# A fused recurrence and expert kernel: the first 768 tokens by plain products, weight sums moved to the second block, first loads from three queues

## Chip, cores, metric

The kernel runs on one core of a Trainium2 chip. The metric is the device time of one execution in microseconds (us), lower is better. Runs are grouped into rounds in which a kernel and the kernel before run on the same chip.

## The reference, cut to what matters

```
sig = 1 / (1 + exp(-f_logit))                 # batch 4, sequence 6080, width 256
f = lower_bound + (1 - lower_bound) * sig
h[t] = f[t] * h[t-1] + (1 - f[t]) * x[t]      # the recurrence; its output y has 24320 rows
hid = y @ w_in                                # 256 -> 2048, w_in arrives in 64-bit floats
g = hid - tanh(hid)
out = g @ w_out                               # 2048 -> 256, w_out in 64-bit floats
```

## The kernel before

Tokens are handled in blocks: one of 256 and 47 of 512. A block has four units u (a quarter of the hidden width each). Both matrix products use a scheme of seven half-size products in place of eight (Winograd's form of Strassen's), which needs four sums of each weight and of the activations. VectorE (DVE) makes these sums, does the recurrence, and takes part in converting the weights from 64-bit patterns to fp32. TensorE (PE) multiplies, ScalarE (ACT) squares and copies, and SP issues the transfers.

Some words for what follows. A mix is one of the sums of activations that the scheme needs. A bank is a piece of PSUM, the memory that PE writes its products to. For g, ScalarE squares a product and forms a quadratic of the square, VectorE makes a factor of it and multiplies the product by that factor (the shrink). This polynomial serves for small values only, so a flag records whether a square was over 0.03, and a general version of the kernel then runs.

```python
def round_weight(n):                 # conversion, then the four sums of the scheme
    ...
    to_float32(dsts, raw[:], temps)  # 5 passes of 1024 columns on DVE, 2 on ScalarE
    A21 = S3                         # the slot of A21 is overwritten by S3
    for o, a, b, op in (
        (S1, A21, A22, ALU.add), (S2, S1, A11, ALU.subtract),
        (S4, A12, S2, ALU.subtract), (S3, A11, A21, ALU.subtract),
    ):
        nc.vector.tensor_tensor(out=w[:, o, :], in0=w[:, a, :], in1=w[:, b, :], op=op)
...
fetch_weight(order[0])               # all on nc.sync: w_in 0,
fetch(0)                             # f_logit and x of the first block (256 tokens),
... lower_bound ...
fetch_weight(order[1])               # w_in 1
...
def need(n):                         # convert and sum when the first product needs it
    while ready <= order.index(n):
        round_weight(order[ready])
        ...
for cycle in range(-1, NBLK + 3):    # one fixed interleaving of all steps of a block
    for name, u, at in turns:
        ...
        if name[0] in "PQ":
            need((int(name[0] == "Q"), u))
        steps[name](j * NU + u)
```

Of the kernel before, what the change touches and what calls it, by code (L numbers as in the profile page):

```python
# [8 lines left out]
FP32 = mybir.dt.float32  # L9
ALU = mybir.AluOpType  # L10
AF = mybir.ActivationFunctionType
# [3 lines left out]
BF16 = mybir.dt.bfloat16  # L15
PSUM = bass.MemoryType.PSUM
P = 128
# [3 lines left out]
TINY = 0.03  # L21
RA, RB, RC = 0.2302117198239662, -0.2895648714772302, 0.24948550042070589
# [8 lines left out]
def kernel(  # L31
# [25 lines left out]
    nc = tc.nc  # L57

    B, S, D = x.shape
    DFF = moe_w_in.shape[1]  # L60
    N = B * S
    KC = D // P
    TB = 512
    HB = TB // 2
    NQ = TB // P
    NU = DFF // TB
    H = 32
    G = P // H
    assert D == 2 * P and DFF == 4 * TB and N % HB == 0

    sizes = [HB] * (N % TB // HB) + [TB] * (N // TB)
    starts = [sum(sizes[:j]) for j in range(len(sizes))]
    NBLK = len(starts)
    srcs = [a.rearrange("b s d -> (b s) d") for a in (f_logit, x)]
# [2 lines left out]
    lb = const.tile([P, KC], FP32, name="lb")  # L77
    om = const.tile([P, KC], FP32, name="om")
    nom = const.tile([P, KC], FP32, name="nom")
    flags = const.tile([P, NBLK * NU * 2], FP32, name="flags")  # L80
# [4 lines left out]



    def fetch_w_in(u, raw):

        src = moe_w_in.rearrange(  # L90
            "(i k a) (s u f) -> i k u a s f", i=G, k=KC, a=H, s=2, u=NU
        )
        dst = raw.rearrange("p (k s f) -> p k s f", k=KC, s=2)
        for i in range(G):
            for k in range(KC):
                nc.sync.dma_start(out=dst[i * H : (i + 1) * H, k], in_=src[i, k, u])  # L96

    def fetch_w_out(u, raw):

        src = moe_w_out.rearrange("(s u c m) d -> u s m c d", s=2, u=NU, c=2, m=P)  # L100
        dst = raw.rearrange("p (s c d) -> p s c d", s=2, c=2)
        for s in range(2):
            nc.sync.dma_start(out=dst[:, s], in_=src[u, s])

    def to_float32(dsts, raw, temps):

# [117 lines left out]
    def fast(ctx):  # L224
# [8 lines left out]
        fetch, steps, ys = recurrence(ctx)  # L233
# [16 lines left out]
        A11, S3, A12, A22, S1, S2, S4 = range(7)  # L250
        raws = {}

        def fetch_weight(n):
            kind, u = n
            raw = rawpool.tile([P, KC * TB], INT64, name="raw")
            (fetch_w_in, fetch_w_out)[kind](u, raw[:])
            raws[n] = raw

        def round_weight(n):
            kind, u = n  # L260
            raw = raws.pop(n)
            temps = [
                rawpool.tile([P, 2, 2, HB], FP32, name=s, tag=s, bufs=1)[:] for s in "emr"
            ]
            w = (w_in, w_out)[kind][u]
            if kind == 0:
                dsts = [(w[:, 0:4, :].rearrange("p n f -> p (n f)"), lambda a: a)]
            else:
                dsts = [
                    (  # L270
                        w[:, 2 * s + k, :].rearrange("p (n a) -> p n a", a=H),
                        lambda t, s=s, k=k: t[:, s * TB : (s + 1) * TB].rearrange(
                            "p (n k a) -> p n k a", k=2, a=H
                        )[:, :, k],
                    )
                    for s in range(2)
                    for k in range(2)
                ]
            to_float32(dsts, raw[:], temps)
            A21 = S3  # L280
            for o, a, b, op in (
                (S1, A21, A22, ALU.add),
                (S2, S1, A11, ALU.subtract),
                (S4, A12, S2, ALU.subtract),
                (S3, A11, A21, ALU.subtract),
            ):
                nc.vector.tensor_tensor(  # L287
                    out=w[:, o, :], in0=w[:, a, :], in1=w[:, b, :], op=op
                )
# [27 lines left out]
        st = {}  # L317
# [98 lines left out]
        acc = {}  # L416
# [117 lines left out]
        for word in around.split():  # L534
            name, u, at = re.fullmatch(r"([a-zA-Z0-9]+)(?:\.(\d))?([+-]\d)?", word).groups()
            turns.append((name, u and int(u), int(at or 0)))


        order = [(0, u) for u in range(NU)] + [(1, u) for u in range(NU)]

        with tc.manual_schedule():
            nc.vector.memset(ones[:], 1.0)
            nc.vector.memset(zeros[:], 0.0)


            bank = ps_b.tile([P, 2, HB], FP32, name="B", tag="B")
            nc.tensor.matmul(
                bank[:], lhsT=zeros[:, 0:P], rhs=zeros[:], start=True, stop=True,
                skip_group_check=True,
            )  # L550
            fetch_weight(order[0])
            fetch(0)
            for i in range(G):
                nc.sync.dma_start(
                    out=lb[i * H : (i + 1) * H, :],
                    in_=lower_bound.rearrange("(i k a) -> i a k", i=G, a=H)[i],
                )
            fetch_weight(order[1])
            nc.vector.tensor_scalar(
                out=om[:], in0=lb[:], scalar1=-1.0, scalar2=1.0,  # L560
                op0=ALU.mult, op1=ALU.add,
            )
            nc.vector.tensor_scalar_add(out=nom[:], in0=lb[:], scalar1=-1.0)
            ready = 0

            def need(n):
                nonlocal ready
                while ready <= order.index(n):
                    round_weight(order[ready])
                    ready += 1  # L570
                    if ready + 1 < len(order):
                        fetch_weight(order[ready + 1])

            for cycle in range(-1, NBLK + 3):
                for name, u, at in turns:
                    j = cycle + at
                    if not 0 <= j < NBLK:
                        continue
                    if u is None:
                        steps[name](j)  # L580
                        if name == "tx" and j + 1 < NBLK:
                            fetch(j + 1)
                        continue
                    if name[0] in "PQ":
                        need((int(name[0] == "Q"), u))
                    steps[name](j * NU + u)
            nc.vector.reduce_max(out=worst[:], in_=flags[:], axis=mybir.AxisListType.X)
            most = ps_b.tile([P, 2, HB], FP32, name="most", tag="D")
            nc.tensor.matmul(
                most[0:1, 0, 0:1], lhsT=worst[:], rhs=ones[:], start=True, stop=True  # L590
            )
            nc.vector.tensor_copy(out=flag[:], in_=most[0:1, 0, 0:1])

    @with_exitstack
    def general(ctx):
# [14 lines left out]
        with tc.manual_schedule():  # L610
            for u in range(NU):
                for fetch_w, w in ((fetch_w_in, w_in[u]), (fetch_w_out, w_out[u])):
                    raw = tpool.tile([P, KC * TB], INT64, name="raw", tag="raw")
                    fetch_w(u, raw[:])
                    to_float32(
                        [(w[:].rearrange("p a b c -> p (a b c)"), lambda a: a)], raw[:],
                        [temp(s)[:] for s in ("t", "q", "th")],
                    )
# [99 lines left out]
```

## Time and profile before

| | before |
|---|---|
| time, median of 3 runs | 2388.83 us (2388.62 to 2389.11) |
| span of the profiled run | 2386.9 us |
| PE busy, DVE busy | 97%, 90% |
| first product | 22.9 us |
| pace of the loop from 148 us on | 48.35 us per 512 tokens, PE without a gap |
| last product to the end of the span | 10.0 us |

The lines themselves are in the prediction below. To read such a profile, take the span apart by the engine that was busy. Here one place repeats in every cycle of the loop, so the loop's pace can be read off exactly. What lies ahead of it and behind it is a remainder that can be explained piece by piece.

### The profile page before, as it was taken

What the parts mean: (1) busy time and instruction counts of PE and PEld (TensorE: products, weight loads), DVE (VectorE), ACT (ScalarE), POOL (GpSimd) and SP (SyncE); (2) the same over time, 40 slices, a digit from 0 to 9 for tenths busy, and PEclk for the clock granted to TensorE, in tenths of its full rate; (3) what the DMA queues carried; (4) which work ended last, traced back from release to release, by engine and by line L of the source; (5) the groups of instructions that cost most, each with busy time, mean ns of one, the idle gap of its engine ahead of it and who ended that gap; (6) DMA issues with size and microseconds to landing.
All of it is one profiled execution on the core that took longest, in us unless ns stands there. A gap on an engine that the chain in (4) does not pass through costs nothing.

```text
span 2386.9 us, 28944 instructions
## 1 busy us (share of the span) xinstructions
PE 2318.5 (97%) x10756; PEld 2040.8 (85%) x10756; DVE 2159.2 (90%) x2496; ACT 1816.9 (76%) x2705; POOL 0.2 (0%) x4
## 2 busy tenths in 40 slices
PE   3699999999999999999999999999999999999998
PEld 2688888888888888888888888888888888888887
DVE  7899899989999999989998999899999999899987
ACT  4578777787777777787787778777777777777775
POOL 0000000000000000000000000000000000000000
PEclk9799999999999999999999999999999999999999
DMA  6211211121112111121112111211111111111101
GB/s 150 54 23 27 45 36 27 27 45 36 27 27 43 30 35 27 34 38 36 27 27 45 36 27 27 45 34 29 27 40 32 36 27 31 41 36 27 27 9 28
DMA packets 306261, 85.07 MB, mean 36 GB/s; under 512 B 302016, under 2 KB 302016, under 8 KB 306112
## 3 DMA queue, kind: packets, MB, share of 16 engines
q1 hardware_dynamic: 306112, 83.14, 16.9%
q8 instruction: 86, 1.41, 0.2%
q14 instruction: 63, 0.52, 0.1%
HBM read 58.20 MB, written 24.90 MB: 35 GB/s over the span
## 4 chain that ended last, share of the span: by engine, by line
PE 96%; DVE 2%; SPq 1%; DMA 0%; ACT 0%; issue 0%; DVEq 0%; ACTq 0%
PE A L344 27%; PE Qa L427 14%; PE Qb L427 14%; PE D L344 14%; PE Qd L427 14%; PE Qc L427 7%; PE B L344 7%; SPq L96 0%; DVE r L126 0%; DVE e L127 0%; SPq L152 0%; DVE w_out L132 0%; DMA xn<-in_x_dram 0%; DVE w_out L287 0%; DVE w_in L287 0%
## 5 line engine op out<-in xcount | busy, mean ns | idle before, releaser
L344 PE MATMUL A<-T,w_in 128*128 128x256 f32 (+1 forms) x2304 | 581.1, 379 | 0.0
L344 PEld LDWEIGHTS A<-T,w_in 128*128 128x128 f32 x2304 | 437.5, 192 | 58.4 <-DVE h L359 0.2
L388 DVE TENSOR_TENSOR h<-h,q 128x1024 f32<-128x1024 f32 (+1 forms) x384 | 452.6, 1211 | 3.3
L382 DVE SCALAR_TENSOR_TENSOR q<-q,t 128x1024 f32<-128x1024 f32 (+1 forms) x384 | 455.2, 1206 | 0.0
L375 ACT ACTIVATE q<-t 128x1024 f32<-128x1024 f32 (+1 forms) x384 | 396.3, 1044 | 46.7 <-DVE h L388 43.6
L372 ACT ACTIVATE t<-h 128x1024 f32<-128x1024 f32 (+1 forms) x384 | 402.6, 1048 | 8.8 <-DVE h L359 5.8
L393 ACT ACTIVATE junk<-t 128x1024 bf16<-128x1024 f32 (+1 forms) x384 | 402.0, 1047 | 1.6
L407 DVE TENSOR_TENSOR Tg<-h 128x512 f32<-128x512 f32 (+2 forms) x384 | 360.4, 939 | 6.8
L427 PE MATMUL Qb<-h,w_out 128*128 128x256 f32 (+1 forms) x1536 | 359.9, 377 | 0.0
L427 PEld LDWEIGHTS Qb<-h,w_out 128*128 128x128 f32 x1536 | 290.2, 190 | 38.9
L427 PE MATMUL Qa<-h,w_out 128*128 128x256 f32 (+1 forms) x768 | 228.6, 380 | 11.5 <-DVE w_out L132 11.5
L344 PE MATMUL A<-y,w_in 128*128 128x256 f32 (+1 forms) x768 | 198.7, 382 | 35.3 <-DVE w_in L132 35.3
L427 PE MATMUL Qa<-Tg,w_out 128*128 128x256 f32 (+1 forms) x768 | 229.2, 381 | 2.6 <-DVE w_out L287 2.6
L356 ACT COPY h<-B 128x512 f32<-128x512 f32 (+1 forms) x192 | 110.9, 578 | 152.6 <-PE B L344 101.9
L356 ACT COPY h<-A 128x512 f32<-128x512 f32 (+1 forms) x192 | 111.1, 579 | 152.2 <-PE A L344 140.3
L427 PE MATMUL Qd<-Tg,w_out 128*128 128x256 f32 (+1 forms) x768 | 226.8, 377 | 0.0
L427 PE MATMUL Qd<-h,w_out 128*128 128x256 f32 (+1 forms) x768 | 226.7, 377 | 0.0
L359 DVE TENSOR_TENSOR h<-D,r 128x512 f32<-128x512 f32 (+1 forms) x192 | 131.4, 684 | 96.3 <-PE D L344 95.4
L427 PE MATMUL Qc<-Tg,w_out 128*128 128x256 f32 (+1 forms) x768 | 195.9, 378 | 7.5 <-DVE w_out L287 7.5
L359 DVE TENSOR_TENSOR h<-A,r 128x512 f32<-128x512 f32 (+1 forms) x192 | 131.0, 682 | 78.2 <-PE A L344 45.6
L344 PE MATMUL D<-y,w_in 128*128 128x256 f32 (+1 forms) x768 | 198.5, 382 | 0.0
L344 PE MATMUL D<-T,w_in 128*128 128x256 f32 (+1 forms) x768 | 197.6, 380 | 0.3 <-DVE h L359 0.3
(55 smaller groups left out, 2836.9 us busy)
## 6 DMA issues: line engine op xcount, KB each, us to landing
fn<-in_f_logit_dram SPq DMA_DIRECT2D x188, 128.0 KB, 3.2
xn<-in_x_dram SPq DMA_DIRECT2D x188, 128.0 KB, 3.3
out_dram<-osb SPq DMA_DIRECT2D x188, 128.0 KB, 2.8
raw<-in_moe_w_in_dram SPq DMA_DIRECT2D x32, 128.0 KB, 3.6
raw<-in_moe_w_out_dram SPq DMA_DIRECT2D x8, 512.0 KB, 4.5
fn<-in_f_logit_dram SPq DMA_DIRECT2D x4, 64.0 KB, 2.9
xn<-in_x_dram SPq DMA_DIRECT2D x4, 64.0 KB, 2.3
out_dram<-osb SPq DMA_DIRECT2D x4, 64.0 KB, 1.9
```

The costliest lines, as they stand in the source:

```text
L344: nc.tensor.matmul(ps[:, c], lhsT=w_in[u][:, slot, c * P : (c + 1) * P], rhs=mixes[j][right], start=start and c == 0, stop=True, skip_grou ...
L356: nc.scalar.copy(out=dst, in_=piece(n, bank))
L359: nc.vector.tensor_tensor(out=piece(n, "h")[:, q], in0=piece(n, bank), in1=piece(n, r), op=ALU.add)
L372: nc.scalar.activation(out=half(n, i, "t"), in_=half(n, i), func=AF.Square)
L375: nc.scalar.activation(out=half(n, i, "q"), in_=half(n, i, "t"), func=AF.Square, scale=RA, bias=RB,)
L382: nc.vector.scalar_tensor_tensor(out=q, in0=q, scalar=RC, in1=t, op0=ALU.add, op1=ALU.mult)
L388: nc.vector.tensor_tensor(out=h, in0=h, in1=q, op=ALU.mult)
L393: nc.scalar.activation(out=junk[:, :, :, 0 : st[n]["hb"]], in_=t, func=AF.Relu, bias=-TINY, accum_out=flags[:, 2 * n + i : 2 * n + i + 1],)
L407: nc.vector.tensor_tensor(out=o, in0=a, in1=b, op=ALU.subtract)
L427: nc.tensor.matmul(acc[j, part][:, r, 0 : st[n]["hb"]], lhsT=w_out[u][:, slot, c * P : (c + 1) * P], rhs=piece(n, right)[:, q, c], start=( ...
```

## The change

Its intent is to shorten the start. PE's first products should not wait for the sums, which then are made while PE works on the second block; and the first data should arrive sooner. Since plain products use eight products for seven, PE gets more work. Cuts are marked.

```diff
-    sizes = [HB] * (N % TB // HB) + [TB] * (N // TB)
+    sizes = [TB] + [HB] * (N % TB // HB) + [TB] * (N // TB - 1)
+    PLAIN = 1 + N % TB // HB
...
+        def plain_first(j, u):       # 8 products of 512 columns, squares from PSUM
+            ...
+        def plain_second(j, u):      # 16 products of 256 columns; the last unit stores
+            ...
         with tc.manual_schedule():
+            fetch(0)
+            fetch_weight((0, 0), nc.scalar)
+            ... lower_bound on nc.gpsimd ...
+            fetch_weight((0, 1), nc.sync)
...
+            ready(0)                 # conversion only, and the next fetch
+            for u in range(NU):
+                plain_first(0, u)
+                for i in {0: (1, 2), 1: (3, 4), 2: (5, 6), 3: (7,)}[u]:
+                    ready(i)
+                if u > 0:
+                    plain_second(0, u - 1)
+                for step in REC[3 * u : 3 * u + 3]:
+                    steps[step](1)
...
+            for u in range(NU):
+                for j in range(1, PLAIN):
+                    plain_first(j, u)
+                ...
+                sum_weight((0, u))
+                if u > 0:
+                    sum_weight((1, u - 1))
+                ... recurrence of block 2 ...
+            if PLAIN > 1:
+                plain_second(1, NU - 1)      # stores block 1
+                if NBLK > 3:
+                    fetch(3)
+            sum_weight((1, NU - 1))
+            for step in ("m13", "m2", "m4"):
+                steps[step](PLAIN)
-            for cycle in range(-1, NBLK + 3):
+            for cycle in range(PLAIN, NBLK + 3):
```

More of the change, by code (lines that the diff above doesn't have):

```diff
@@ L84, with fetch_w_in @@
     zeros = const.tile([P, TB], FP32, name="zeros")
-    def fetch_w_in(u, raw):
+    def fetch_w_in(u, raw, queue):
         src = moe_w_in.rearrange(
@@ L95, in fetch_w_in, with fetch_w_out @@
             for k in range(KC):
-                nc.sync.dma_start(out=dst[i * H : (i + 1) * H, k], in_=src[i, k, u])
-    def fetch_w_out(u, raw):
+                queue.dma_start(out=dst[i * H : (i + 1) * H, k], in_=src[i, k, u])
+    def fetch_w_out(u, raw, queue):
         src = moe_w_out.rearrange("(s u c m) d -> u s m c d", s=2, u=NU, c=2, m=P)
@@ L102, in fetch_w_out @@
         for s in range(2):
-            nc.sync.dma_start(out=dst[:, s], in_=src[u, s])
+            queue.dma_start(out=dst[:, s], in_=src[u, s])
     def to_float32(dsts, raw, temps):
@@ L251, in fast, with fetch_weight @@
         raws = {}
-        def fetch_weight(n):
+        def fetch_weight(n, queue):
             kind, u = n
             raw = rawpool.tile([P, KC * TB], INT64, name="raw")
-            (fetch_w_in, fetch_w_out)[kind](u, raw[:])
+            (fetch_w_in, fetch_w_out)[kind](u, raw[:], queue)
             raws[n] = raw
@@ L279, in round_weight, with sum_weight @@
             to_float32(dsts, raw[:], temps)
+        def sum_weight(n):
+            kind, u = n
+            w = (w_in, w_out)[kind][u]
             A21 = S3
@@ L536, in fast @@
             turns.append((name, u and int(u), int(at or 0)))
-        order = [(0, u) for u in range(NU)] + [(1, u) for u in range(NU)]
-        with tc.manual_schedule():
+        def plain_first(j, u):
+            nb = sizes[j]
+            n = j * NU + u
+            gT = hpool.tile([P, 2, 2, TB], FP32, name="h", tag="h")
+            st[n] = gT
+            for s in range(2):
+                banks = []
+                for c in range(2):
+                    pool, name = ((ps_a, "A"), (ps_b, "B" if c == 0 else "D"))[s]
+                    bank = pool.tile([P, TB], FP32, name=name, tag=name)
+                    banks.append(bank)
+                    for k in range(KC):
+                        nc.tensor.matmul(
+                            bank[:, 0:nb],
+                            lhsT=w_in[u][:, 2 * k + s, c * P : (c + 1) * P],
+                            rhs=ys[j][:, k, 0:nb],
+                            start=(k == 0),
+                            stop=(k == KC - 1),
+                        )
+                t, q = [
+                    tpool.tile([P, 2, TB], FP32, name=name, tag=name)[:, :, 0:nb]
+                    for name in "tq"
+                ]
+                for c in range(2):
+                    nc.scalar.activation(
+                        out=t[:, c], in_=banks[c][:, 0:nb], func=AF.Square
+                    )
+                nc.scalar.activation(out=q, in_=t, func=AF.Square, scale=RA, bias=RB)
+                nc.vector.scalar_tensor_tensor(
+                    out=q, in0=q, scalar=RC, in1=t, op0=ALU.add, op1=ALU.mult
+                )
+                for c in range(2):
+                    nc.vector.tensor_tensor(
+                        out=gT[:, s, c, 0:nb], in0=banks[c][:, 0:nb], in1=q[:, c],
+                        op=ALU.mult,
+                    )
+                junk = sumpool.tile([P, 2, TB], BF16, name="junk", tag="junk")
+                nc.scalar.activation(
+                    out=junk[:, :, 0:nb], in_=t, func=AF.Relu, bias=-TINY,
+                    accum_out=flags[:, 2 * n + s : 2 * n + s + 1],
+                )
@@ new lines, in plain_second @@
+        def plain_second(j, u):
+            nb = sizes[j]
+            ns = nb // P
+            gT = st.pop(j * NU + u)
+            if u == 0:
+                acc[j] = [
+                    ps_b.tile([P, 2, D], FP32, name=f"Q{b}", tag=f"Q{b}")
+                    for b in ("ab" if j == 0 else "c")[0 : (ns + 1) // 2]
+                ]
+            for s in range(2):
+                for c in range(2):
+                    for i in range(ns):
+                        nc.tensor.matmul(
+                            acc[j][i // 2][:, i % 2].rearrange("p (k m) -> p k m", k=2),
+                            lhsT=gT[:, s, c, i * P : (i + 1) * P],
+                            rhs=w_out[u][:, 2 * s : 2 * s + 2, c * P : (c + 1) * P],
+                            start=(u == s == c == 0 and i % 2 == 0),
+                            stop=(u == NU - 1 and s == c == 1),
+                            skip_group_check=True,
+                        )
+            if u == NU - 1:
+                osb = opool.tile([P, NQ, D], FP32, name="osb", tag="osb")
+                for i in range(ns):
+                    nc.scalar.copy(
+                        out=osb[:, i].rearrange("p (i k a) -> p k i a", k=2, a=H),
+                        in_=acc[j][i // 2][:, i % 2].rearrange(
+                            "p (k i a) -> p k i a", k=2, a=H
+                        ),
+                    )
+                nc.sync.dma_start(
+                    out=out[starts[j] : starts[j] + nb, :].rearrange(
+                        "(i p) d -> p i d", p=P
+                    ),
+                    in_=osb[:, 0:ns, :],
+                )
@@ L542, in fast, with ready @@
+        REC = ("tf", "sg", "tx", "f0", "v0", "sc0", "f1", "v1", "sc1")
+        with tc.manual_schedule():
+            fetch(0)
+            fetch_weight((0, 0), nc.scalar)
+            for i in range(G):
+                nc.gpsimd.dma_start(
+                    out=lb[i * H : (i + 1) * H, :],
+                    in_=lower_bound.rearrange("(i k a) -> i a k", i=G, a=H)[i],
+                )
+            fetch_weight((0, 1), nc.sync)
             nc.vector.memset(ones[:], 1.0)
             nc.vector.memset(zeros[:], 0.0)
+            nc.vector.tensor_scalar(
+                out=om[:], in0=lb[:], scalar1=-1.0, scalar2=1.0,
+                op0=ALU.mult, op1=ALU.add,
+            )
+            nc.vector.tensor_scalar_add(out=nom[:], in0=lb[:], scalar1=-1.0)
+            for step in REC:
+                steps[step](0)
+            fetch(1)
+            order = [(0, 0), (0, 1), (1, 0), (0, 2), (1, 1), (0, 3), (1, 2), (1, 3)]
+            def ready(i):
+                round_weight(order[i])
+                if i + 2 < len(order):
+                    fetch_weight(order[i + 2], nc.sync)
+            ready(0)
[7 more added lines that the diff above has]
+                    steps[step](1)
+            if NBLK > 2:
+                fetch(2)
+            for u in range(NU):
+                for j in range(1, PLAIN):
+                    plain_first(j, u)
+                if u == 0:
+                    plain_second(0, NU - 1)
+                elif PLAIN > 1:
+                    plain_second(1, u - 1)
+                sum_weight((0, u))
+                if u > 0:
+                    sum_weight((1, u - 1))
+                if PLAIN > 1:
+                    for step in REC[3 * u : 3 * u + 3]:
+                        steps[step](2)
+            if PLAIN > 1:
+                plain_second(1, NU - 1)
[4 more added lines that the diff above has]
+                steps[step](PLAIN)
@@ L550, in fast @@
             )
-            fetch_weight(order[0])
-            fetch(0)
-            for i in range(G):
-                nc.sync.dma_start(
-                    out=lb[i * H : (i + 1) * H, :],
-                    in_=lower_bound.rearrange("(i k a) -> i a k", i=G, a=H)[i],
-                )
-            fetch_weight(order[1])
-            nc.vector.tensor_scalar(
-                out=om[:], in0=lb[:], scalar1=-1.0, scalar2=1.0,
-                op0=ALU.mult, op1=ALU.add,
-            )
-            nc.vector.tensor_scalar_add(out=nom[:], in0=lb[:], scalar1=-1.0)
-            ready = 0
-            def need(n):
-                nonlocal ready
-                while ready <= order.index(n):
-                    round_weight(order[ready])
-                    ready += 1
-                    if ready + 1 < len(order):
-                        fetch_weight(order[ready + 1])
-            for cycle in range(-1, NBLK + 3):
+            for cycle in range(PLAIN, NBLK + 3):
                 for name, u, at in turns:
                     j = cycle + at
-                    if not 0 <= j < NBLK:
+                    if not PLAIN <= j < NBLK:
                         continue
                     if u is None:
+                        if (j, name) == (PLAIN, "m4"):
+                            continue
                         steps[name](j)
@@ L583, in fast @@
                         continue
-                    if name[0] in "PQ":
-                        need((int(name[0] == "Q"), u))
                     steps[name](j * NU + u)
@@ L613, in general @@
                     raw = tpool.tile([P, KC * TB], INT64, name="raw", tag="raw")
-                    fetch_w(u, raw[:])
+                    fetch_w(u, raw[:], nc.sync)
                     to_float32(
```

## The prediction

> **What bounds the kernel now.** I read the page's busy times first, then the slices and the chain that ended last, then busy time by stage, the waits of the first 150 us, and the timeline of the start and the end.
>
> ```profile
> PE 2318.5 (97%) x10756; PEld 2040.8 (85%) x10756; DVE 2159.2 (90%) x2496; ACT 1816.9 (76%) x2705; POOL 0.2 (0%) x4
> PE   3699999999999999999999999999999999999998
> PEclk9799999999999999999999999999999999999999
> PE 96%; DVE 2%; SPq 1%; DMA 0%; ACT 0%; issue 0%; DVEq 0%; ACTq 0%
> ```
>
> Over the whole run TensorE (PE) sets the time, with VectorE (DVE) close behind; only the first two slices (60 us each) have PE below 9 tenths. So anything to gain without touching the loop lies there. By stage (columns: stretch, its length, then busy us and instructions of PE, PEld, DVE, ACT, POOL, then clock, DMA share, GB/s):
>
> ```profile
> 0.00:22.93 22.93, 2.08 (x3) 0.50 (x3) 9.59 (x18) 4.90 (x6) 0.20 (x4) 1.00 0.68 148
> 22.93:97.94 75.01, 41.80 (x201) 38.20 (x202) 66.33 (x110) 39.09 (x73) 0.00 (x0) 0.80 0.51 116
> 97.94:147.97 50.03, 45.34 (x225) 40.04 (x225) 46.23 (x62) 38.40 (x57) 0.00 (x0) 0.97 0.12 22
> 147.97:196.32 48.35, 48.35 (x226) 42.56 (x225) 43.73 (x50) 37.80 (x57) 0.00 (x0) 1.00 0.14 28
> 2323.41:2386.90 63.49, 53.88 (x251) 47.04 (x249) 48.58 (x56) 34.85 (x51) 0.00 (x0) 0.95 0.12 27
> ```
>
> The cuts from 97.94 on are the same place of successive cycles of the loop. From 147.97 a 512-token block costs 48.35 us and PE never idles; in the second stretch PE works 42 of 75 us and DVE 66 of 75. So the start is bound by DVE, the rest by PE. The last stretch holds 124 pairs of matmul instructions; at 0.432 us a pair (48.35/112 pairs per block) that is 53.5 us, so PE also runs full to 2376.9 and a drain of 10.0 us follows. What PE waits for in the start (columns: us in total, times, longest), and the first weights in order of time:
>
> ```profile
> PE A L344 <- DVE w_in L132: 35.3, 4, 19.4
> PE Qa L427 <- DVE w_out L132: 11.5, 3, 4.1
> PE Qc L427 <- DVE w_out L287: 7.5, 1, 7.5
> ...
> 13.53 0.17 DVE L559 TENSOR_SCALAR om<-lb 128x2 f32<-128x2 f32 x1 [12.11 <-DMA lb<-in_lower_bound_dram]
> ...
> 21.65 1.23 DVE L132 SCALAR_TENSOR_TENSOR w_in<-r,e 128x1024 f32<-128x1024 f32 x1
> ...
> 22.93 0.80 PE L344 MATMUL A<-y,w_in 128*128 128x128 f32 x2 [19.38 <-DVE w_in L132]
> ```
>
> PE waits for weights (conversion from 64-bit floats, about 5.2 us of DVE for each of eight pieces, then 1.68 us of sums); DVE's first work waits for lower_bound, issued last by the one queue. An account of the 2386.9 us: full-rate work of 47 blocks at 48.35 and the 256-token block at 24.2 is 2296.6; 22.9 before the first product; 10.0 drain; the remaining 57.4 are stalls and slow clock in the start. That 57.4 plus 22.9 is what the change can attack.
>
> **What the Trainium skill says.** "VectorE: DVE Perf Modes", section "The TRN2 errata", gives (N+151)/0.96 ns for an fp32 tensor_tensor: 1224 ns for N=1024, 691 for 512. The trace has 1226 for the conversion's add and 0.69 us for 512 columns from PSUM, so I use trace durations for the new DVE rows. "TensorE: Matmul & The Clock Gate", Part 1, says the idle array runs at half rate until about 3.4 us of activity and falls back after an idle window of that length. The trace agrees: 128-column instructions start 0.215 us apart at 31.9 us and 0.11 apart at 102.6, and the clock of the second stretch is 0.80. "DMA: Bandwidth & Descriptors", section "Issuing engines are not separate DMA queues", says several queues save only the sequencer's issue time; here eight w_in issues took SP 5.17 us, and lower_bound landed only at 13.5.
>
> **The change, part by part.** *PE work.* A plain unit has 8+8 full products where the seven-product scheme has 7+7, so a block costs 48.35 x 8/7 = 55.3 us. The 512-token plain block adds 6.9 and the 256-token one (27.6 against 24.2) adds 3.4. Full-rate work becomes 55.3 + 27.6 + 46 x 48.35 = 2307.0, which is 10.4 more. This is paid for sure.
>
> *DVE work until the loop starts.* Recurrence of 512 tokens 6.5 (two transposes 1.24, two products 0.75, two scans 1.28); eight conversions 41.6; shrinks of block 0: 8 x (1.21 + 2 x 0.69) = 20.7; recurrence of 256 tokens 3.5; shrinks of block 1: 8 x (0.68 + 2 x 0.42) = 12.2; recurrence of the third block 6.5; sums 8 x 1.68 = 13.4; mixes 1.5. Sum 105.9. The joins and spreads of the scheme are gone for 768 tokens, and no product waits for a sum.
>
> *First product.* f_logit and x of 512 tokens go first on SP (issued by about 5 us, landing 3.3 later), w_in 0 in parallel on ACT (landed by 9 to 10), lower_bound on GpSimd. DVE should start near 7 to 8 instead of 13.5. It then has 6.5 of recurrence, about 5.2 of conversion and a little waiting for x: first product at 20.3. The doubled first block eats most of the earlier start, so only 2.6 us are won.
>
> *Walk through the queues.* I placed each engine's instructions in its program order with the durations above. Unit (0,0) runs on a cold PE; its chain PE, square, quadratic, factor, shrink ends on DVE at 34. Only then come w_in 1 (39.0) and w_out 0 (44.1), so unit (0,1) starts at 39.0. In the same way unit (0,2) starts at 58.7, (0,3) at 75.1, block 1 at 88.9; each period is 10.3 of conversion, 5.2 of shrink, the rest ACT latency. PE needs 13.8 of each 16 to 20. In block 1 the units alternate 3.45 us products of both layers with DVE shrinks and sums; DVE finishes the mixes at 130.4, PE starts the loop at 128. Check: DVE from 8 with 105.9 of work would be done at 114, so the walk holds 16 us of waits. Weight loads stay hidden: two raw buffers, and by my walk each piece lands 3 us or more before its conversion.
>
> *Loop and end.* 46 blocks x 48.35 = 2224.1. In the first cycle no second-layer work of an older block fills PE, and it waits for copies and joins: walking it gives 3 us lost by the next block's first product. Drain 10.0 as before. Sum: 128 + 2224.1 + 3 + 10 = 2365; as an account, 20.3 + 82.9 + 25 stalls + 3 + 2224.1 + 10. The measured time is 1.9 above the span (2388.8 and 2386.9), so **2367 us**, 22 less or 0.9%. Of the 57.4 of stall and slow clock 28 remain; 10.4 of the gain is spent on the extra products.
>
> **Rivals.** (1) *The clock becomes the bound.* The plain start has PE gaps of 3 to 9 us between units, and at half rate a unit takes 27.6 instead of 13.8, more than DVE's 16. For it: the clock of 0.80 in the stretch of before, and 0.50 in its 60 to 70 us window. Against: products come in runs of 7 to 14 us, long enough to warm up. A clock of 0.7 throughout would cost about 15 us (2382); half rate for all of block 0 would bring 40 and a time near 2405, slightly slower than before. (2) *DVE saturated.* If ACT latencies overlap better than in my walk, the loop starts near 114 and the time is 2353. For it: 66 of 75 us busy in before with a similar mix. Against: the new DVE order puts conversions behind each unit's shrink, which waits for PE and ACT in series. (3) *Loads late.* 3 MB now start at once on shared engines; at the 148 GB/s of the first 23 us, the 2 MB needed for the first product take 14 us, so it would start near 24: 2371. DMA share 0.68 there leaves room, so I hold this for a small term. (4) *Ramp larger.* If the loop's first cycle takes its whole 48.35 for lack of overlap, 10 us are lost instead of 3: 2374.
>
> **Range and chances.** The loop's pace and the drain are measured; uncertain are the loop's start (rivals 1 to 3, about 8 us either way) and the ramp (up by 7). That gives 2357 to 2379. A gain over 2% needs a time below 2341, a loop start near 102, below even the DVE-saturated 114: 1 in 100. Slower by over 2% needs 48 us of new stalls, more than half rate throughout: 1 in 200. Within 2% is left with 0.985.
>
> **What would show each step.** First product near 20; the second unit's near 39; TensorE clock 0.8 to 0.95 and DVE about 85% busy between 20 and 128; the first seven-product matmul at about 128; blocks from there at 48.35 us; drain 10.0 us. Right mechanism with a wrong size is a loop start off by over 8 us. The argument is wrong if PE, not DVE, is the busy engine in the start, if block time in the loop moves from 48.35, or if PE waits there for a DMA of raw weights.

## More of the kernel before

All runs quoted here are fast ones. The experiments ran on several chips; the medians of the kernel before lay between 2388.14 and 2388.96 there.

## The result

The changed kernel takes 2375.29 us (median of 6 runs, 2372.12 to 2378.24), against 2388.47 us for the kernel before in the same rounds. Ratios here are the mean time of one kernel's fast runs over that of the other's of the same rounds, so not quite the ratio of the medians. The ratio is 0.9944 (95% interval 0.9931 to 0.9956): faster by 0.6%, inside 2%, and inside the predicted range of 2357 to 2379. The profiled run's span is 2374.0 us. The page of the changed kernel, answering the first lines of the prediction:

```profile
PE 2316.8 (98%) x10628; PEld 2020.9 (85%) x10628; DVE 2130.6 (90%) x2456; ACT 1801.3 (76%) x2685; POOL 2.5 (0%) x8
PE   4999999999999999999999999999999999999997
PEclk9999999999999999999999999999999999999999
PE 95%; DVE 2%; DMA 1%; ACT 1%; issue 0%; SPq 0%; DVEq 0%
```

In the start only the first slice has PE below 9 tenths now (the last one holds the end), and DMA has 1% of the chain that ended last, where it had 0%. Busy time by stage of the changed kernel (columns as in the prediction), cut at the first product, the second block's first product and the loop's first product:

```profile
0.00:25.00 25.00, 0.00 (x0) 0.00 (x0) 11.89 (x15) 5.74 (x6) 2.45 (x8) 1.00 0.88 148
25.00:96.36 71.36, 55.94 (x161) 32.89 (x162) 55.58 (x72) 41.70 (x57) 0.00 (x0) 0.90 0.39 103
96.36:131.78 35.42, 35.42 (x163) 30.70 (x162) 30.22 (x63) 19.09 (x49) 0.00 (x0) 1.00 0.04 15
131.78:180.00 48.22, 43.25 (x197) 36.70 (x196) 40.74 (x50) 38.27 (x58) 0.00 (x0) 1.00 0.34 66
```

In the first block DVE and PE are busy for nearly the same time (55.6 and 55.9 us of 71.4), so neither is saturated. From the first product to the loop PE is busy for 91.4 of 106.8 us and DVE for 85.8. In the second block PE has no gap at all. The first 48 us of the loop hold gaps of 5 us. The waits of the first 150 us of the changed kernel (total, times, longest), and below them the waits of SP's queue:

```profile
PE A L557 <- DVE w_in L134: 40.4, 4, 25.0
...
DVE q L573 <- ACT q L572: 18.4, 12, 7.7
...
DVE xT L163 <- DMA xn<-in_x_dram: 6.5, 2, 3.8
```
```profile
SPq L154 <- DMA raw<-in_moe_w_in_dram: 5.6, 7, 3.6
```

No product waits for a sum any more; PE waits for four conversions of w_in. DVE waits for ScalarE's quadratic, and for x.

The account of the prediction, now with what was measured. PE's last product starts at 2361.36 and fills its place by 2361.8. Loop work is 46 x 48.35 = 2224.1.

| us | before | predicted | changed |
|---|---|---|---|
| first product at | 22.9 | 20.3 | 25.0 |
| PE's work at full rate | 2296.6 | 2307.0 | 2307.0 |
| stalls and slow clock after the first product, before the loop | 57.4 (with first cycle) | 25 | 23.9 (131.78 - 25.0 - 82.9) |
| lost in the loop's first cycle | | 3 | 5.9 (2361.8 - 131.78 - 2224.1) |
| last product to end of span | 10.0 | 10.0 | 12.2 |
| span | 2386.9 | 2365 | 2374.0 |

So stalls fell from 57.4 to 29.8, a gain of 27.6. Of it 10.4 went to the additional products, 2.1 to a later first product and 2.2 to a longer end. What remains is 12.9.

### The profile page after: what moved, and what is told of

Same layout as the page of the kernel before. It is cut to its first block, busy times and chain, and to the rows that moved or that the text cites. A ratio compares the mean times of both kernels' runs of the same rounds, so it can differ in the third digit from the quotient of the medians.

```text
span 2374.0 us, 28606 instructions
## 1 busy us (share of the span) xinstructions
PE 2316.8 (98%) x10628; PEld 2020.9 (85%) x10628; DVE 2130.6 (90%) x2456; ACT 1801.3 (76%) x2685; POOL 2.5 (0%) x8
## 4 chain that ended last, share of the span: by engine, by line
PE 95%; DVE 2%; DMA 1%; ACT 1%; issue 0%; SPq 0%; DVEq 0%
PE A L350 26%; PE Qd L433 13%; PE Qb L433 13%; PE Qa L433 13%; PE D L350 13%; PE Qc L433 7%; PE B L350 7%; PE A L557 1%; DMA raw<-in_moe_w_in_dram 1%; PE Qb L600 0%; PE Qa L600 0%; DVE q L573 0%; DVE w_out L293 0%; PE D L557 0%; PE B L557 0%; DVE h L577 0%
## 5 line engine op out<-in xcount | busy, mean ns | idle before, releaser
L350 PE MATMUL A<-T,w_in 128*128 128x256 f32 x2208 | 559.2, 379 | 2.0 <-ACT r L362 1.8
L394 DVE TENSOR_TENSOR h<-h,q 128x1024 f32<-128x1024 f32 x368 | 437.3, 1219 | 3.2
L388 DVE SCALAR_TENSOR_TENSOR q<-q,t 128x1024 f32<-128x1024 f32 x368 | 439.7, 1216 | 0.0
L381 ACT ACTIVATE q<-t 128x1024 f32<-128x1024 f32 x368 | 382.7, 1052 | 45.3 <-DVE h L394 42.4
L378 ACT ACTIVATE t<-h 128x1024 f32<-128x1024 f32 x368 | 388.6, 1056 | 4.8 <-DVE h L365 2.0
L399 ACT ACTIVATE junk<-t 128x1024 bf16<-128x1024 f32 x368 | 388.1, 1055 | 1.5
L413 DVE TENSOR_TENSOR Tg<-h 128x1024 f32<-128x1024 f32 x368 | 347.9, 945 | 6.5
L433 PE MATMUL Qb<-h,w_out 128*128 128x256 f32 x1472 | 347.7, 379 | 0.0
L433 PE MATMUL Qa<-Tg,w_out 128*128 128x256 f32 x736 | 218.9, 379 | 0.0
L433 PE MATMUL Qd<-h,w_out 128*128 128x256 f32 x736 | 218.9, 379 | 0.0
```

Source lines behind the costliest of these rows:

```text
L350: nc.tensor.matmul(ps[:, c], lhsT=w_in[u][:, slot, c * P : (c + 1) * P], rhs=mixes[j][right], start=start and c == 0, stop=True, skip_grou ...
L378: nc.scalar.activation(out=half(n, i, "t"), in_=half(n, i), func=AF.Square)
L381: nc.scalar.activation(out=half(n, i, "q"), in_=half(n, i, "t"), func=AF.Square, scale=RA, bias=RB,)
L388: nc.vector.scalar_tensor_tensor(out=q, in0=q, scalar=RC, in1=t, op0=ALU.add, op1=ALU.mult)
L394: nc.vector.tensor_tensor(out=h, in0=h, in1=q, op=ALU.mult)
L399: nc.scalar.activation(out=junk[:, :, :, 0 : st[n]["hb"]], in_=t, func=AF.Relu, bias=-TINY, accum_out=flags[:, 2 * n + i : 2 * n + i + 1],)
```

## The experiments

The theory after the comparison has four parts. (a) The plain blocks carry the gain. (b) The three queues do not make the start earlier; x arrives late, and GpSimd's queue costs time at the end. (c) In the first block a chain sets the pace: product, square, quadratic, shrink, and only then the next conversions, because they stand behind the shrinks in DVE's queue. A half-rate clock after PE's gaps adds to it. (d) From the conversion of w_in 3 on, PE is the bound, up to a wait for late loads in the loop's first cycle. The rivals: the queues make the gain; DVE's total work bounds the start; the clock does not matter; the loop's first cycle is slow for lack of overlap. Ten kernels were run, all with the right result, each with 5 rounds. Of the edits made alone to the changed kernel, only the conversions between products and shrinks have an interval clear of the changed kernel's 0.9931 to 0.9956. The other intervals overlap it, so in those runs the trace has to carry the reading and the time alone does not.

### One queue again

```diff
-            fetch_weight((0, 0), nc.scalar)
-            ... lower_bound on nc.gpsimd ...
+            ... lower_bound on nc.sync ...
+            fetch_weight((0, 0), nc.sync)
```

> The changed kernel with all initial loads on the one queue again, in the order f_logit and x of the first block, lower_bound, w_in 0, w_in 1. Theory A (the three-queue start made x late: its four transfers were issued only at 7.4 us after waiting for other transfers, and landed at 14.6): x is issued by about 5.5 us and lands near 9.5, the first product moves from 25.0 to about 21.5 us, the time from 2375 to about 2372. Theory B (issuing from several queues is what makes the start early): w_in 0 lands later, the first product stays at 25 or moves to 28, time 2375 to 2379. If the GpSimd queue is behind the longer stretch from the last DVE work to the end of the span (9.1 us after the flag copy against 6.8 before), that stretch falls back to about 7.

Measured: 2369.72 us (2367.85 to 2372.11), ratio to before 0.9924 (0.9910 to 0.9937), 5.6 us under the changed kernel. The start of the changed kernel, with three queues (start, duration, engine, line, operation, and the idle time before it):

```profile
0.75 2.98 SPq L154 DMA_DIRECT2D fn<-in_f_logit_dram  x4
0.75 6.73 ACTq L98 DMA_DIRECT2D raw<-in_moe_w_in_dram  x8
7.36 2.49 SPq L154 DMA_DIRECT2D xn<-in_x_dram  x4
14.63 1.25 DVE L163 STREAM_TRANSPOSE xT<-xn 128x1024 f32<-128x1024 f32 x1 [3.84 <-DMA xn<-in_x_dram]
```

And with one queue:

```profile
0.73 1.98 SPq L154 DMA_DIRECT2D fn<-in_f_logit_dram  x4
2.75 2.08 SPq L154 DMA_DIRECT2D xn<-in_x_dram  x4
6.81 10.23 SPq L98 DMA_DIRECT2D raw<-in_moe_w_in_dram  x16
10.97 1.20 DVE L163 STREAM_TRANSPOSE xT<-xn 128x1024 f32<-128x1024 f32 x1
```

With three queues SP issued f_logit and then stood still until 7.36, waiting for transfers of w_in (the wait of 3.6 us shown above). The kernel's text asks for no such wait; where it comes from is not shown. With one queue x is out by 4.83 and transposed 3.7 us earlier, and the first product starts at 21.31. w_in 0 is issued later, but still arrives before it is needed. The loop starts at 125.78, 6.0 earlier: 3.7 from the first product, and the rest from products of block 0 that happened to run faster this time (A of the first unit 5.14 us against 5.89, of the last 3.70 against 5.23), which the edit does not explain. The stretch from the end of the flag copy to the end of the span fell from 9.1 to 6.8 us. The traces bear out theory A.

### A warm clock

```diff
+            idle = ps_b.tile([P, 2, D], FP32, name="Qc", tag="Qc")
             for u in range(NU):
+                for _ in range((25, 9, 3, 2)[u]):
+                    nc.tensor.matmul(idle[:], lhsT=zeros[:, 0:P], rhs=zeros[:], ...)
                 plain_first(0, u)
```

> The changed kernel with products of zeros (25, 9, 3 and 2 of them) put into PE's gaps before each unit of the first block, into a bank not yet in use. Theory A (half-rate clock after each gap delays the first products of units 0, 2 and 3 by about 2 us each, on the path to the conversion of w_in 3 and then on PE itself): units' A products take 3.5 us instead of 5.2 to 5.9, the loop starts about 5.8 us earlier (126), time near 2369.5, with less spread between runs. Theory B (DVE's work alone sets the pace): A products get faster but the loop's start stays at 131.8, time 2375.

Measured: 2371.79 us (2370.95 to 2372.25), ratio 0.9931 (0.9917 to 0.9944). The products into A of the four units, in the changed kernel and then with the zero products:

```profile
25.00 5.89 PE L557 MATMUL A<-y,w_in 128*128 128x512 f32 x8 [25.00 <-DVE w_in L134]
43.61 5.13 PE L557 MATMUL A<-y,w_in 128*128 128x512 f32 x8 [9.28 <-DVE w_in L134]
62.83 5.40 PE L557 MATMUL A<-y,w_in 128*128 128x512 f32 x8 [3.75 <-DVE w_in L134]
80.95 5.23 PE L557 MATMUL A<-y,w_in 128*128 128x512 f32 x8 [2.38 <-DVE w_in L134]
```
```profile
25.34 3.60 PE L557 MATMUL A<-y,w_in 128*128 128x512 f32 x8
41.65 3.70 PE L557 MATMUL A<-y,w_in 128*128 128x512 f32 x8 [1.56 <-DVE w_in L134]
60.89 5.30 PE L557 MATMUL A<-y,w_in 128*128 128x512 f32 x8 [2.62 <-DVE w_in L134]
78.91 3.70 PE L557 MATMUL A<-y,w_in 128*128 128x512 f32 x8 [0.66 <-DVE w_in L134]
```

Eight instructions take 3.7 us when warm and 5.1 to 5.9 when cold. The zero products warmed three units of four, and the loop started at 128.20, 3.6 us earlier. That is less than the 5.8 expected: the third unit stayed cold after a gap of 2.62 us. The spread between runs fell from 6.1 to 1.3 us. Over all kernels with plain blocks, those whose mean clock is 0.997 or more (this one and three below) spread by 0.2 to 1.3 us and the others by 3.2 to 6.1. This agrees with a clock that falls differently from run to run in the changed kernel, but no run separates the causes of the spread. The clock is on the path; it is not the main term.

### Three of four sums made early

```diff
                 round_weight(order[i])
+                sums(order[i], (0, 1, 2))     # S1, S2, S4 at once; S3 as in the change
```

> The changed kernel with three of the four sums of each weight made right after its conversion, in the first block, so that part of the change is undone; the total of DVE work is the same. Theory A (DVE and its waits set the pace up to the conversion of w_in 3 at 81 us, PE without a gap from there to the loop at 131.8): four sums of 1.25 us come onto the path before w_in 3, the DVE time freed in the second block buys nothing, the loop starts about 5 us later, time near 2380. Theory B (DVE is the bound over the whole start): total work unchanged, so 2375.

Measured: 2379.08 us (2377.80 to 2381.99), ratio 0.9963 (0.9949 to 0.9976), 3.8 us over the changed kernel; the intervals of the two ratios just overlap. The profiled run agrees with the mechanism: the first product starts 0.7 us earlier than in the changed kernel (24.27), the fourth unit 2.7 later (83.63 against 80.95), so some 3.4 of the 5 expected came onto the path. Where the rest went is not shown, since the products also ran at another clock (A of the second unit 6.71 us against 5.13). The freed DVE time in the second block bought no earlier loop, which starts at 134.28 against 131.78. In its first cycle the wait for the mixes is gone, but one for ScalarE's copies has grown to 5.0 us, because DVE, with its mixes done sooner, waits 7.5 us for f_logit of block 3, the late load that the next experiment moves. Equal total work in another place gave a longer time, which speaks against a start bound by DVE's total.

### Loads of block 3 ahead of the store of block 1

```diff
                     for step in REC[3 * u : 3 * u + 3]:
                         steps[step](2)
+                    if u == 0 and NBLK > 3:
+                        fetch(3)
...
                 plain_second(1, NU - 1)
-                if NBLK > 3:
-                    fetch(3)
```

> The changed kernel with the loads of block 3 issued once block 2 is transposed, ahead of the store of block 1 on the queue, instead of after it. Theory A (the loop's first cycle lost 5.9 us, not the 3 predicted, because DVE waited 2.2 and 2.7 us for these loads, issued at 132 behind the store): the loss falls to about 3, time near 2372.5. Theory B (the loss is copies, joins and the mix of the new block): the waits for loads go, the PE gaps stay, time 2375.

Measured: 2369.69 us (2368.65 to 2371.84), ratio 0.9923 (0.9909 to 0.9937). The loop's first products in the changed kernel:

```profile
134.45 1.13 PE L350 MATMUL D<-T,w_in 128*128 128x256 f32 x4 [1.64 <-DVE T L320]
...
137.50 1.25 DVE L163 STREAM_TRANSPOSE fT<-fn 128x1024 f32<-128x1024 f32 x1 [2.19 <-DMA fn<-in_f_logit_dram]
...
138.78 1.06 ACT L172 ACTIVATE fT<-fT 128x1024 f32<-128x1024 f32 x1 [2.58 <-DVE fT L163]
...
140.85 1.99 PE L350 MATMUL A<-T,w_in 128*128 128x256 f32 x8 [1.81 <-ACT r L362]
```

And with the loads early:

```profile
134.02 1.13 PE L350 MATMUL D<-T,w_in 128*128 128x256 f32 x4 [1.64 <-DVE T L320]
...
134.80 1.24 DVE L163 STREAM_TRANSPOSE fT<-fn 128x1024 f32<-128x1024 f32 x1
...
138.44 1.89 PE L350 MATMUL A<-T,w_in 128*128 128x256 f32 x8
```

PE's wait of 1.81 was for a copy on ScalarE. That copy stood behind a sigmoid, the sigmoid behind a transpose, and the transpose behind a load that SP could issue only after the store of block 1. With the loads early the loss in the first cycle falls from 5.9 to 1.9 us (PE's last product starts at 2356.97, the loop at 131.36). In the profiled runs the gain is 4.2 us, in the medians 5.6; the rest is within the spread of the changed kernel. Theory A holds for the loads, and the 1.64 us for the mixes remain.

### Conversions between products and shrinks

```diff
-                plain_first(0, u)
-                for i in {0: (1, 2), 1: (3, 4), 2: (5, 6), 3: (7,)}[u]:
-                    ready(i)
+                plain_first(0, u, {0: (1, 2), 1: (3, 4), 2: (5, 6), 3: (7,)}[u])
...                                    # inside plain_first
+            for i in between[0:1]:    # after the products, ahead of squares and shrinks
+                ready(i)
             ... squares, quadratics, shrinks of both halves ...
+            for i in between[1:]:
+                ready(i)
```

> The changed kernel with each unit's conversions moved in the program order of DVE and ScalarE: one right after the unit's products, ahead of its squares and shrinks, and one after both shrinks (in the changed kernel both come after the shrinks). Same work. Theory A (what holds the start is DVE standing idle for the chain product, square, quadratic while the next weights wait behind it in its queue, 18 us in the changed kernel): the next w_in is ready before PE has finished the unit, PE's waits for w_in after the first fall from 15.4 us to under 5, its clock stays full, the loop starts near 121 instead of 131.8, time near 2365. Theory B (DVE's work itself or ScalarE is the bound, or the loads of raw weights come too late for the new order): loop start within 3 us of 131.8, time 2372 to 2376, with new waits for raw weights.

Measured: 2364.27 us (4 runs, 2363.91 to 2364.89), ratio 0.9900 (0.9885 to 0.9915), 11.0 us under the changed kernel. The first products of the second and third unit of this run:

```profile
33.92 3.70 PE L557 MATMUL A<-y,w_in 128*128 128x512 f32 x8 [0.33 <-DVE h L580]
...
51.08 3.70 PE L557 MATMUL A<-y,w_in 128*128 128x512 f32 x8 [1.48 <-DVE h L580]
```

They start 9.7 and 11.8 us earlier than in the changed kernel. Waits for w_in are gone but for the first; PE waits instead up to 1.8 us for a bank that the shrinks have to free. From the second unit on the clock stays full. The loop starts at 120.02. DVE is now busy for 54.5 of the first block's 59.5 us. The same work in another order gave the largest gain of any single edit, so theory A holds: the start was held by order, not by the amount of work. The edit moves the conversions in ScalarE's queue as well as in DVE's, and no run separates the two. The gain also holds the full clock: in the changed kernel the A products of these three units took 4.7 us more than here.

### Each part of the change alone

```diff
# the kernel before with the loads of the change
-            fetch_weight(order[0])
-            fetch(0)
-            ... lower_bound on nc.sync ...
-            fetch_weight(order[1])
+            fetch(0)
+            fetch_weight(order[0], nc.scalar)
+            ... lower_bound on nc.gpsimd ...
+            fetch_weight(order[1], nc.sync)
```

> The kernel before with only the loads of the change: f_logit and x first, w_in 0 from ScalarE's queue, lower_bound from GpSimd's, w_in 1 after. Theory A (later conversions and sums, not the first loads, set the start of before, and the GpSimd queue costs 2.3 us at the end): first product earlier by 1 to 3 us, end of PE earlier by up to 2, time 2387 to 2390. Theory B (the three queues carry the gain of the change): time 2376 to 2382.

```diff
# the changed kernel with the loads of before
-            fetch(0)
-            fetch_weight((0, 0), nc.scalar)
-            ... lower_bound on nc.gpsimd ...
+            fetch_weight((0, 0), nc.sync)
+            fetch(0)
+            ... lower_bound on nc.sync ...
             fetch_weight((0, 1), nc.sync)
```

> The changed kernel with the loads as they were: one queue, order w_in 0, f_logit and x, lower_bound, w_in 1. So the plain blocks alone. Theory A (the gain is the plain blocks', the three queues add nothing): DVE starts near 13.7, first product near 25.5, the end 2.3 us shorter without the GpSimd queue, time 2372 to 2375, no worse than the changed kernel. Theory B (the queues make the early start): first product at 28 or later, time 2378 to 2382.

| us | loads of before | loads of the change |
|---|---|---|
| blocks of before | 2388.14 (9 runs) | 2386.34 (2385.65 to 2387.43) |
| plain blocks | 2376.16 (2373.35 to 2377.94) | 2375.29 (other rounds) |

The ratio of the loads alone is 0.9992 (0.9979 to 1.0006), that of the plain blocks alone 0.9950 (0.9936 to 0.9963). So the plain blocks carry the gain and the queues add nothing that is clear of noise.

In the first kernel the first product came 3.6 us earlier (19.35) and PE ended 5.1 earlier, more than the 2 expected. The end of the span became 2.8 us longer (12.8 from PE's last product), so its time is still only just below the 2387 to 2390 expected. In the second the first product came at 27.73, between the two expectations. lower_bound arrived only at 16.1 there, 2.4 later than I had assumed, and so DVE started late. The three queues thus start the first product 2.7 us sooner than the old loads, and give back 2.2 at the end.

### What GpSimd's queue costs at the end

```diff
# lower_bound only, from nc.gpsimd to nc.sync; w_in 0 stays on nc.scalar
-                nc.gpsimd.dma_start(out=lb[...], in_=...)
+                nc.sync.dma_start(out=lb[...], in_=...)
```

> The changed kernel with only the four lower_bound loads moved from GpSimd's queue to SP's, after x; w_in 0 stays on ScalarE's. Theory A (the use of GpSimd's queue costs 2.3 us between the copy of the flag and the end of the span): that stretch is 6.8 to 7 us instead of 9.1; lower_bound lands later (at 11 to 12), but x, which lands at 14, still sets the recurrence, so the first product stays at 25 or moves by less than 1 us and the time is near 2373. Theory B (the stretch varies for other reasons): it stays at 9.1, time 2375 or more.

Measured: 2372.84 us (2372.47 to 2375.64), ratio 0.9940 (0.9926 to 0.9953). The last instruction that counts as work in the changed kernel, whose span is 2374.0, and in this run, whose span is 2371.0:

```profile
2364.77 0.15 DVE L710 COPY flag<-most 1x1 f32<-1x1 f32 x1 [0.37 <-PE most L707]
```
```profile
2363.94 0.15 DVE L710 COPY flag<-most 1x1 f32<-1x1 f32 x1 [0.37 <-PE most L707]
```

The stretch after it is 9.1 us with GpSimd's queue and 6.9 without. All six profiled kernels that used that queue have 9.1 to 9.7, and all six without it 6.8 to 6.9. The cost is shown; which step of the program's end takes it is not. lower_bound landed later than expected (DVE began at 14.27), and the first product started at 25.91. SP's x was still issued only at 6.86, so it is not GpSimd's queue that held it.

### Together

> Three edits together: one queue with x first (5.6 us gained alone), loads of block 3 ahead of the store (5.6 alone, 4.0 of them in the loop's first cycle), conversions between the products and the shrinks. If they add up: first product 21.3, loop start near 117, first-cycle loss near 2, end shorter by 2.3, time near 2354. If they share a cause or the loop's first cycle turns DVE-bound: 2358 to 2362.

The edits are those of the one queue, the early loads and the conversions in between. Measured: 2354.48 us (4 runs, 2354.38 to 2354.71), ratio 0.9859 (0.9844 to 0.9874). The first product starts at 21.30, the loop at 116.31, and 1.9 us are lost in its first cycle. The gains nearly add up (5.6, 5.6 and 11.0 are 22.2; measured 20.8, in other rounds).

A last run adds 19 zero products before the first unit and puts the mixes ahead of the last sum:

```diff
+            for _ in range(19):
+                nc.tensor.matmul(idle[:], lhsT=zeros[:, 0:P], rhs=zeros[:], ...)
...
-            sum_weight((1, NU - 1))
             for step in ("m13", "m2", "m4"):
                 steps[step](PLAIN)
+            sum_weight((1, NU - 1))
```

> The three edits of the run that had all of them, and two more: 19 products of zeros on PE before the first unit (its A products took 5.1 us at half rate), and the mixes of block 2 put before the last sum of weights on DVE (PE waited 1.6 us for the first of them at the loop's start). If both stand on the path: loop's second product 1.6 us earlier, unit 1 earlier by up to 1.5, time 2351.5 to 2353. If DVE's own work is the bound by now in the first block (54.5 busy of 58.8 us there): only the mixes count, 2353.

Measured: 2352.69 us (4 runs, 2352.57 to 2352.80), ratio 0.9850 (0.9835 to 0.9865), faster than before by 1.5% and the best of all kernels here. The second unit started 1.5 us earlier (28.70 against 30.20) and the loop 1.5 earlier (114.82). The wait for the mixes went, but the loop's first cycle still loses 1.9 us: PE now waits there for a copy on ScalarE. So of the two edits only the warm clock moved the end, which neither expectation had. The time fits both and does not tell them apart.

## Why the prediction was right

**What bounds.** "The start is bound by DVE, the rest by PE" held for the loop, whose pace did not change. For the new start it was half right. The prediction named as a sign against itself that PE, not DVE, is the busy engine there, and narrowly that came true: PE was busy for 86% from the first product to the loop and DVE for 80% (85% was forecast), at a clock that made PE's products longer. The prediction's walk kept the distinction between DVE's work and DVE's waits, and the run with conversions in between shows that it mattered: filling those waits, with the full clock that came with it, was worth 11 us.

**Added work, 10.4 us.** Paid in full, as predicted: PE ran the second block without a gap, in the 35.4 us of full rate (27.6 of its own and 6.9 of block 0's last second layer, plus one zero product).

**Walk through the first block.** Predicted starts of the four units and of the second block were 20.3, 39.0, 58.7, 75.1, 88.9; measured 25.0, 43.6, 62.8, 81.0, 96.4. From first product to loop the prediction has 107.7 us, the run 106.8. That they agree is luck, since errors cancelled inside it: the third and the last unit took 18.1 and 15.4 us where the walk had 16.4 and 13.8, and the second block had no stalls where the walk had placed 3.7 us. For the last unit the walk had not charged cold products.

**First product, 20.3.** This term of the sum was mis-sized: it came at 25.0. The step that failed is "f_logit and x of 512 tokens go first on SP (issued by about 5 us, landing 3.3 later)". x was issued at 7.36 and used at 14.63. Rival 3, which gave 24 for this, was nearer in the number. Its cause, transfers that share bandwidth, is not separated from the wait of SP's queue: GB/s in the first stretch was 148 before and after. I had called it a small term because DMA share left room in the profile before, but that share belonged to one queue in order. The run with one queue has x where the prediction wanted it, and its first product at 21.31.

**Loop's first cycle, 3 us.** Mis-sized: 5.9. The walk took the loads of block 3 for granted. The run with early loads brought 1.9.

**Drain "10.0 as before".** Wrong by 2.2: GpSimd's queue lengthens the end, as shown without it.

**The sum.** The loop began 3.8 later than predicted, its first cycle lost 2.9 more, the end was 2.2 longer: 8.9, which is the span's 2374.0 against 2365. All three errors went the same way, and the range held them, but of the 22 us forecast only 13 came. **Rival 1**, the clock, was real and small: the clock granted in the first block was 0.90, and the zero products brought 3.5 us. The record of the clock even flatters: it shows 1.00 from 25 to 30 us, where the A products took 5.89 us instead of 3.70. **Rival 2** did not happen by itself, but the run with conversions in between reached what it described for the first block.

Three smaller slips change nothing: w_in 1 was issued after lower_bound, which so was not the last; the last slice before also has PE below 9 tenths; and 48 us is the distance from the kernel before to 2% slower, while from the predicted time it is 70.

## What to carry to other kernels

When work is moved to hide a wait, look at where it stands in the queue of the engine that does it: here DVE waited up to 7.7 us for ScalarE with conversions standing behind that wait. In this start reordering the same work gained 11 us, and queues for loads should be added only after asking what each issue waits for. Walk an in-order schedule through with measured durations and check the terms nobody disputes as well, the drain and the next block's loads, since those were the ones missed.

## What the Trainium skill lacked or had wrong

- "DMA: Bandwidth & Descriptors", section "Issuing engines are not separate DMA queues", says that several queues save only the sequencer's issue time. Here they did not even save that for the transfer that mattered: SP's x was issued at 7.36 us after a wait for another queue's transfers, against 2.75 with one queue, and the eight issues on ScalarE took 6.73 us where eight on SP took 5.17 before. The section does not say that issues of one queue can come to wait on completions of another, as they did in this program (why is not shown).
- No page has the cost of GpSimd's queue at the end of a program: 9.1 to 9.7 us from the last instruction that counts as work to the end of the span with it, 6.8 to 6.9 without.
- "TensorE: Matmul & The Clock Gate", Part 1, ties the fall to half rate to an idle window of about 3.4 us. Here gaps of 2.4 and 2.6 us were followed by slow products in some runs (5.23 and 5.30 us for eight instructions), and in others a gap of 2.4 us was not (3.70 us). A subsection of that Part on short idles between groups of products has no length for them.
